# One order for five engines, searched anew: RWKV attention followed by a squared-ReLU MLP on one NeuronCore

## The chip, the cores and the metric

The kernel runs on 1 core of one Trainium2 chip. The metric is the device time of one execution, in microseconds (us). The core has five instruction streams that matter here: PE (TensorE, matmuls and transposes through matmul), DVE (VectorE), ACT (ScalarE), POOL (GpSimd) and SP (SyncE, which only starts DMAs). Each stream runs in order; semaphores hold an instruction until what it needs is done.

## The reference

Four sequences of 768 tokens, 8 heads of 48 channels, go through a linear attention with a decayed state, and the result (3072 tokens of 384 channels) through an MLP with a squared ReLU:

```python
for t in range(S):
    cur = np.einsum('bhd,bhe->bhde', u[None] * kt, vt)
    y[:, :, t] = np.einsum('bhd,bhde->bhe', rt, state + cur)
    state = wt[:, :, :, None] * state + np.einsum('bhd,bhe->bhde', kt, vt)
...
h = x @ w_in            # 384 x 2048
r = np.maximum(h, 0.0)
g = r * r
return g @ w_out        # 2048 x 384
```

## The kernel before, in words

The 3072 tokens are cut into 12 steps of 256 tokens, three to a sequence. A step s is written as a set of words, and each word issues one operation (or a few of one kind) on one engine. The order of all 864 words is written out by hand, in the string ORDER (L17), and a loop at the end of the kernel (L598) issues them one after the other. So ORDER fixes, for each engine, the order of its own instructions; between engines only the data and the buffers decide. A word reads `name.step.index`; `=A`, `=V` or `=G` behind it puts it on ACT, DVE or POOL, and `:n` names the PSUM bank or banks that it writes.

The words of one step, in the order of the data:

- ld (L172): DMAs of w, r, k, v into a ring of four steps; `ld.g.i` and `ld.g.o` (L188, L194) load the four chunks of the two MLP weights in f32, and cast (L200) makes them bf16.
- ww, rw, kw, ku, qp (L262 to L302): elementwise products of f32 tiles in SBUF, two tensor operands each; q (L306) sums over channels; lw (L268) takes a logarithm; v, vs, qs (L272, L281, L311) are copies that rearrange; vq (L316) is a product of two SBUF tiles.
- cum (L321, PE) sums the logarithms; al (L333), exp, ac (ACT) and rd (L351, DVE, rd.s.0 for r and rd.s.1 for k) turn them into decayed r and k. They read the bank that cum wrote, so that bank is free for the next user only after rd.
- The decayed r and k are transposed: in steps 0 to 3 by PE (tr, L370, copied out by rkt, L386), in steps 4 to 11 by a DMA transpose on SP (dtr, L397).
- p (L409, PE) and pm (L423, DVE, product with a mask out of PSUM): the scores; su (L436, PE), ts (L450), sn (L458, POOL): the state; y and yc (L475, L486, PE): the output; ysb (L499, DVE) adds vq to it.
- The output is transposed for the MLP: in steps 0 to 5 by PE and a copy (yt L509, xt L518), in steps 6 to 11 by a DMA transpose (dyt, L523).
- m1.s.g (L529, PE, six matmuls) makes 2 of 16 blocks of hidden channels; rl (L541, ACT or DVE) evicts them with the ReLU; sq (L549) squares two rl in SBUF; m2.s.c.q (L559, PE, four matmuls) adds a quarter of the hidden channels to 128 tokens of the result; os (L567) evicts it, store (L575) writes it out.
- warm (L579) are matmuls on a zero tile, issued while the first data comes.

PSUM has eight banks: att0 and att1 (two banks each, used by cum, p, su, y) and the four of `quad`, of which 0 and 1 are called `b` and 2 and 3 `m`. In the order before, m1 uses banks 2 and 3 in turn, and m2 banks 0 and 1. p, su and yc are matmuls on tiles of 64 x 64 of the array; y, m1, m2, tr, yt and cum use all of it.

Of the kernel before, what the change touches and what calls it, by code (L numbers as in the profile page):

```python
# [35 lines left out]
qp_.3=G ld.5.v m1_.2.3:2 os_.0.0=V rl_.2.0=V tr_.3.1:0 rl_.2.3=A tr_.3.0:1 rkt_.3.1=V v_.3=A ld.4.r m1_.2.4:3
ww_.4=G rkt_.3.0=V m2_.1.0.0:0 rl_.2.4=A q_.3 ww_.5=G p_.3.1:0 vs_.3.1=A ld.6.k su_.3:1 pm_.3.1 p_.3.0:m
m2_.1.0.1 ts_.3.0=A lw_.4 sn_.3.0 ld.5.k pm_.3.0 m2_.1.0.2 qs_.3=A m2_.1.1.0:1 sq_.2.0=A vq_.3=G ts_.3.1=V
m2_.1.0.3 ld.6.w cum_.4:0 m2_.1.1.1 ku_.4=G ac_.4 al_.4 store.0.1 m1_.2.5:2 os_.1.0=A v_.5=A yc_.3.1:1 y_.3:1
lw_.5 kw_.4=G m1_.2.2:3 ld.6.r ysb_.3=V rl_.2.5=A m2_.1.1.2 exp_.4 sn_.3.1 rl_.2.2=V yt_.3:0 rw_.4=G cum_.5:1  # L40
xt_.3=V m2_.1.1.3 vs_.4.0=A ac_.5 sq_.2.1=A qp_.4=G al_.5 m1_.3.0:2 rd_.4.1 v_.4=A m1_.3.3:3 rd_.4.0 dtr_.4.1
m2_.2.0.0:0 rl_.3.0=A rw_.5=G rl_.3.3=A m2_.2.0.1 os_.1.1=V exp_.5 q_.4 dtr_.4.0 su_.4:0 sq_.2.2=A m1_.3.4:2
kw_.5=G rd_.5.0 ww_.6=G m2_.2.1.0:1 rl_.3.4=A ts_.4.0=V sq_.2.3=A m1_.3.5:3 vs_.4.1=A rd_.5.1 sn_.4.0
m2_.2.1.1 store.1.0 ts_.4.1=V rl_.3.5=V ku_.5=G m1_.3.6:2 store.1.1 m2_.2.1.2 qs_.4=A ld.7.w ld.6.v rw_.6=G
p_.4.1:1 rl_.3.6=A p_.4.0:0 pm_.4.1 pm_.4.0 m2_.2.1.3 lw_.6 vq_.4=G m1_.3.1:3 m1_.3.2:2 rl_.3.1=A su_.5:1
dtr_.5.1 dtr_.5.0 vs_.5.1=G sq_.3.0=A rl_.3.2=V yc_.4.0:0 yc_.4.1:0 sn_.4.1 y_.4:0 os_.2.1=V sq_.3.1=A
m1_.3.7:3 ysb_.4=V ld.7.v m2_.2.0.2 rl_.3.7=A ld.8.w kw_.6=G vs_.5.0=G yt_.4:1 ld.7.k sq_.3.3=A m2_.2.0.3
xt_.4=V cum_.6:0 al_.6 m1_.4.4:2 qp_.5=G os_.2.0=A ac_.6 m1_.4.7:3 ts_.5.0=V exp_.6 rl_.4.4=V m2_.3.0.0:1
rl_.4.7=A rd_.6.1 m1_.4.6:2 rd_.6.0 m2_.3.0.1 dtr_.6.1 m2_.3.1.0:0 ku_.6=G qp_.6=G sq_.3.2=A rl_.4.6=A q_.5
dtr_.6.0 p_.5.0:1 p_.5.1:0 vs_.6.0=A m1_.4.5:3 sn_.5.0 m2_.3.0.2 qs_.5=G rl_.4.5=A pm_.5.1 pm_.5.0 vq_.5=G  # L50
m1_.4.1:2 m1_.4.3:3 rl_.4.3=A store.2.1 ld.8.v m2_.3.0.3 rl_.4.1=V ld.8.k v_.6=A ww_.7=G y_.5:0 q_.6 os_.3.0=A
ld.7.r m1_.4.0:3 store.0.0 ld.9.k ww_.8=G yc_.5.0:0 qs_.6=A su_.6:1 yc_.5.1:0 ysb_.5=V vs_.6.1=A ts_.6.0=V
m1_.4.2:2 ld.8.r m2_.3.1.1 rl_.4.0=V yt_.5:1 xt_.5=V sn_.6.0 lw_.7 vq_.6=G rl_.4.2=A p_.6.0:0 m2_.3.1.2
sq_.4.3=A store.2.0 pm_.6.0 m1_.5.2:3 ku_.7=G m1_.5.6:2 ts_.6.1=V yc_.6.1:0 sq_.4.0=A rl_.5.2=A p_.6.1:1
rl_.5.6=A m2_.3.1.3 kw_.7=G pm_.6.1 sq_.4.2=A m1_.5.4:3 rw_.7=G m1_.5.3:2 os_.3.1=V rl_.5.4=A y_.6:0 sn_.6.1
rl_.5.3=A cum_.7:1 kw_.8=G ysb_.6=V al_.7 m2_.4.0.0:1 vs_.7.1=A m1_.5.7:3 m1_.5.5:2 v_.7=G dyt_.6 sq_.4.1=A
rl_.5.7=V qp_.7=G rl_.5.5=V m2_.4.1.0:0 exp_.7 ld.9.w ld.9.v m2_.4.0.1 ac_.7 rd_.7.0 sq_.5.1=A m2_.4.0.2
ku_.8=G rd_.7.1 sq_.5.3=A dtr_.7.0 m2_.4.0.3 m1_.5.0:3 lw_.8 m1_.5.1:2 rw_.8=G rl_.5.0=V su_.7:0 q_.7
rl_.5.1=A cum_.8:1 dtr_.7.1 m1_.6.3:3 qs_.7=A m1_.6.5:2 rl_.6.3=V ld.10.w qp_.8=G ac_.8 sq_.5.0=A m2_.4.1.1
os_.4.0=V ts_.7.0=V ld.11.w sn_.7.0 m1_.6.4:3 rl_.6.5=A al_.8 ww_.9=G m2_.4.1.2 ld.9.r rl_.6.4=V exp_.8  # L60
# [574 lines left out]
```

## Time and profile before

| | us |
|---|---|
| three runs: median (lowest to highest) | 182.38 (181.91 to 182.72) |
| the profiled execution, its time | 182.57 |
| the profiled execution, its span (first to last instruction) | 180.8 |

| engine | busy us | share of the span |
|---|---|---|
| PE matmul | 171.2 | 95% |
| ACT | 132.4 | 73% |
| DVE | 129.7 | 72% |
| POOL | 122.8 | 68% |

The granted clock of TensorE is full over the whole span. A row of a timeline reads: start in us, duration, engine, line, operation, output<-inputs, shape, number of instructions, and in brackets the idle time ahead of it with what ended it. A matmul's recorded duration runs longer than the distance to the next start, since matmuls are pipelined; distances are read from start to start. A row of the groups reads: line, engine, operation, tiles, shape, count, then total busy us and mean ns of one, then the idle time ahead of the group and what ended most of it. In the chain of work that ended last, 33% of the span is m2 (L564) and 33% is m1 (L536).

### The profile page before, as it was taken

What the parts mean: (1) busy time and instruction counts of PE and PEld (TensorE: products, weight loads), DVE (VectorE), ACT (ScalarE), POOL (GpSimd) and SP (SyncE); (2) the same over time, 40 slices, a digit from 0 to 9 for tenths busy, and PEclk for the clock granted to TensorE, in tenths of its full rate; (3) what the DMA queues carried; (4) which work ended last, traced back from release to release, by engine and by line L of the source; (5) the groups of instructions that cost most, each with busy time, mean ns of one, the idle gap of its engine ahead of it and who ended that gap; (6) DMA issues with size and microseconds to landing.
All of it is one profiled execution on the core that took longest, in us unless ns stands there. A gap on an engine that the chain in (4) does not pass through costs nothing.

```text
span 180.8 us, 5682 instructions
## 1 busy us (share of the span) xinstructions
PE 171.2 (95%) x2382; PEld 123.2 (68%) x2385; DVE 129.7 (72%) x195; ACT 132.4 (73%) x235; POOL 122.8 (68%) x140
## 2 busy tenths in 40 slices
...
GB/s 147 270 261 232 221 369 350 340 332 302 228 271 217 280 228 215 208 218 255 270 137 237 197 287 101 303 141 143 190 106 244 92 47 0 92 151 22 0 87 130
DMA packets 78952, 35.81 MB, mean 198 GB/s; under 512 B 72144, under 2 KB 77392, under 8 KB 78928
## 3 DMA queue, kind: packets, MB, share of 16 engines
...
## 4 chain that ended last, share of the span: by engine, by line
PE 78%; SPq 10%; DMA 5%; ACT 4%; DVE 1%; issue 1%; ACTq 0%
PE bk L564 33%; PE m L536 33%; SPq L180 8%; DMA w_st<-in_moe_w_in_dram 5%; PE att L420 3%; PE att L483 3%; PE att L493 2%; PE att L446 1%; ACT gt L545 1%; PE bk L516 1%; PE att L328 1%; ACT wi_sb L202 1%; SPq L190 1%; SPq L207 1%; ACT gt L553 1%
## 5 line engine op out<-in xcount | busy, mean ns | idle before, releaser
L536 PE MATMUL m<-xT,wi_sb 128*128 128x256 bf16 x576 | 74.0, 273 | 0.8 <-ACT gt L545 0.7
L564 PE MATMUL bk<-wo_sb,gt 128*128 128x384 bf16 x384 | 72.0, 326 | 0.0
L536 PEld LDWEIGHTS <-wi_sb 128*128 128x128 bf16 x576 | 54.8, 98 | 12.5 <-issue 0.9
L564 PEld LDWEIGHTS <-gt 128*128 128x128 bf16 x384 | 36.9, 98 | 19.2
L545 ACT ACTIVATE gt<-m 128x512 f16<-128x512 f32 x56 | 32.9, 594 | 21.6 <-PE m L536 21.1
L553 ACT ACTIVATE gt<-gt 128x1024 bf16<-128x1024 f16 x42 | 43.3, 1051 | 1.4 <-DVE gt L547 1.1
L547 DVE TENSOR_SCALAR gt<-m 128x512 f16<-128x512 f32 x40 | 27.1, 687 | 9.6 <-PE m L536 9.3
L434 DVE TENSOR_TENSOR pmT<-att,mask 128x1024 bf16<-128x1024 f32 x20 | 23.9, 1218 | 3.9 <-PE att L420 3.9
L299 POOL TENSOR_TENSOR ku<-k_raw,u_bc 128x768 f32<-128x768 f32 x12 | 21.8, 1819 | 0.4 <-DMA u_bc<-in_u_dram 0.4
L304 POOL TENSOR_TENSOR ku<-ku,r_raw 128x768 f32<-128x768 f32 x11 | 20.6, 1877 | 0.2
L318 POOL TENSOR_TENSOR ku<-v_sh,qs 128x768 f32<-128x768 bf16 x11 | 16.2, 1477 | 4.9 <-ACT qs L279 4.8
L279 ACT CAST v_sh<-v_raw 64x384 bf16<-64x384 f32 x34 | 17.3, 508 | 0.4
L292 POOL TENSOR_TENSOR k_raw<-k_raw,w_raw 128x384 f32<-128x384 f32 x12 | 12.1, 1010 | 6.3 <-DMA k_raw<-in_k_dram 6.2
L461 POOL TENSOR_TENSOR S<-t_state,ac_buf 128x192 bf16<-128x192 f32 x20 | 10.2, 508 | 8.1 <-DVE t_state L456 5.7
L504 DVE TENSOR_TENSOR y_sb<-att,ku 128x768 bf16<-128x768 f32 x12 | 11.4, 954 | 5.5 <-PE att L483 1.7
L288 POOL TENSOR_TENSOR r_raw<-r_raw,w_raw 128x384 f32<-128x384 f32 x12 | 12.0, 997 | 3.6 <-DMA r_raw<-in_r_dram 3.6
L363 DVE TENSOR_TENSOR kdec_buf<-k_raw,att 128x768 bf16<-128x768 f32 x12 | 11.4, 950 | 3.5 <-ACT att L342 2.9
L360 DVE TENSOR_TENSOR rdec_buf<-r_raw,att 128x384 bf16<-128x384 f32 x24 | 12.2, 548 | 2.2 <-ACT ac_buf L348 1.1
L342 ACT ACTIVATE att<-att 128x768 f32<-128x768 f32 x12 | 9.6, 799 | 3.4 <-PE att L330 2.0
L571 ACT ACTIVATE o_sb<-bk 128x384 f32<-128x384 f32 x13 | 6.2, 484 | 7.3 <-PE bk L564 7.3
L309 DVE TENSOR_REDUCE q<-ku 128x16 f32<-128x768 f32 x12 | 11.3, 944 | 0.0
L581 PE MATMUL att<-warm 128*128 128x512 bf16 x27 | 8.9, 487 | 1.2 <-DVE half_ones L230 1.2
...
## 6 DMA issues: line engine op xcount, KB each, us to landing
...
```

The costliest lines, as they stand in the source:

```text
L180: nc.sync.dma_start(out=t[:, hs, at:at + 2, :].rearrange("p h j d -> p h (j d)"), in_=src[b, hs, i * T:(i + 1) * T, :].rearrange("h (p j) ...
L279: copy(out[j * Q:(j + 1) * Q, c], src[c * Q:(c + 1) * Q, :, j])
L299: tensor_mul("ku_", s, h)(tiles["ku", s][:, hs], raw["k", s][:, hs, 1:3, :], u_bc[:, hs, None, :].to_broadcast([C, n, 2, D]))
L304: tensor_mul("qp_", s, h)(ku, ku, raw["r", s][:, heads(h), 0:2, :])
L318: tensor_mul("vq_", s)(vq[:], tiles["vs", s][:], tiles["qs", s][:, :, :, None].to_broadcast([C, 2, H, D]))
L360: nc.vector.tensor_mul(rdec[0][:, ps, j, :, 0:D], x[:, :, j, :].rearrange("p (a e) d -> p a e d", e=2), dec.rearrange("p (a e) d -> p a e ...
L434: nc.vector.tensor_mul(pmT, ps_p[:].rearrange("p e (x t) -> p (e x) t", t=C), mk.to_broadcast([C, 8, C]))
L536: nc.tensor.matmul(ps1[:, j, :], wi_sb[:, n // 4, kk, n % 4 * 128:(n % 4 + 1) * 128], tiles["xT", s][:, :, kk, :], start=(kk == 0), stop=( ...
L545: nc.scalar.activation(rl, m1, AF.Relu, scale=RS)
L547: nc.vector.tensor_scalar(out=rl, in0=m1, scalar1=RS, scalar2=0.0, op0=ALU.mult, op1=ALU.max)
L553: nc.scalar.activation(gt, rl, AF.Square)
L564: nc.tensor.matmul(m2, gt[:, 4 * q + n, c * C:(c + 1) * C], wo_sb[:, 4 * q + n, :], start=(summed[s, c] == 1 and n == 0), stop=(summed[s, ...
```

## The change

Only the string ORDER is changed. It holds the same 864 words before and after: the same operations on the same tiles, the same 22 DMA transposes, the same loads and stores. The first 90 words are the same; behind them the sequence is another one, found by a search whose plan of the DMA engines also holds the fetches of instructions and the DMA transposes. Three things differ:

- the sequence of the words on every engine, SP's included;
- the banks: m1 and m2 now take any of the four quad banks (m1: 19, 26, 25 and 26 words on banks 0 to 3, before 0, 0, 48 and 48; m2: 6, 8, 5 and 5 sums, before 11, 13, 0 and 0), tr and yt too, and the quarters of an m2 sum come in any order;
- the engine of 107 words. To DVE go ku.5, ku.10, ku.11, kw.3, kw.8, rw.5, ww.10, vq.2 and vq.9 from POOL, v.5 from ACT, vs.2.1 from POOL, vs.8.0 and vs.11.0 from ACT, and the squares sq.0.0, sq.0.3, sq.2.3, sq.8.0 and sq.10.1 from ACT (sq.9.3 goes to ACT), and ts.3.0 from ACT. 22 rl go from ACT to DVE and 27 the other way, three rkt, two xt and, on balance, one os from DVE to ACT; five qs, four v and four vs go from ACT to POOL, two qs, three v and three vs from POOL to ACT, and cast.o.2 from POOL to ACT.

The diff, cut to the start, to two places in steps 6 to 11, and to the end. First the old lines of these places, then the new ones:

```diff
-ac_.2 cast.i.1=A rd_.2.1 warm_.10.1 tr_.2.0:1 sn_.1.0 p_.1.0:0 ku_.2=G ts_.1.1=V yc_.1.1:1 tr_.2.1:0
-cast.i.0=A pm_.1.0 ld.0.o m1_.0.3:2 ld.3.w rkt_.2.1=V m1_.0.2:3 vq_.1=G rkt_.2.0=V y_.1:1 rl_.0.3=A yc_.1.0:1
-rl_.0.2=V p_.2.0:0 m1_.0.1:2 ld.1.o ysb_.1=V cast.i.2=G m1_.0.0:3 rl_.0.1=A pm_.2.0 yt_.1:0 ld.3.r rl_.0.0=A
-m1_.0.5:2 v_.2=A xt_.1=V qp_.2=G sn_.1.1 m1_.0.4:3 rl_.0.5=A p_.2.1:1 su_.2:b sq_.0.0=A rl_.0.4=V ld.2.o
-m1_.1.4:2 cast.i.3=G ts_.2.0=V pm_.2.1 m1_.1.5:3 rl_.1.4=A q_.2 sn_.2.0 m1_.1.3:2 rl_.1.5=A ld.3.o vs_.2.1=G
-vs_.2.0=A yc_.2.0:0 yc_.2.1:0 rl_.1.3=V m1_.1.6:3 cast.o.0=G qs_.2=A m1_.1.0:2 ld.3.k rl_.1.6=V sq_.0.2=A
-y_.2:0 rl_.1.0=V m1_.1.1:3 vq_.2=G m1_.1.7:2 rl_.1.1=V ld.3.v m2_.0.1.0:0 sq_.1.2=A rl_.1.7=V sq_.0.1=A
-cast.o.1=G m1_.1.2:3 rl_.1.2=A ysb_.2=V m1_.0.7:2 ld.4.w ww_.3=G yt_.2:1 rl_.0.7=V m1_.0.6:3 xt_.2=V m2_.0.1.1
-sq_.1.1=A rl_.0.6=V ld.5.w m1_.2.6:2 cast.o.2=G lw_.3 sq_.1.0=A rl_.2.6=A cum_.3:1 sq_.1.3=A rw_.3=G al_.3
...
-store.3.0 m2_.5.1.0:1 sq_.5.2=A rd_.8.1 ts_.7.1=V sn_.7.1 m1_.6.0:2 vs_.7.0=G vs_.9.1=A rd_.8.0 m2_.4.1.3
-m2_.5.1.1 kw_.9=G rl_.6.0=A dtr_.8.0 p_.7.1:0 v_.8=A p_.7.0:1 vq_.7=G pm_.7.1 m1_.6.1:3 m2_.5.1.2 rl_.6.1=A
-pm_.7.0 ku_.9=G m2_.5.1.3 sq_.6.0=A lw_.9 m1_.6.6:2 dtr_.8.1 store.3.1 q_.8 yc_.7.0:0 v_.9=A yc_.7.1:0
-rl_.6.6=V rw_.9=G su_.8:1 y_.7:0 os_.5.1=A ts_.8.0=V m1_.6.2:3 ysb_.7=V os_.4.1=A cum_.9:1 m1_.6.7:2 al_.9
-dyt_.7 m2_.5.0.0:1 rl_.6.2=V exp_.9 ww_.10=G rl_.6.7=V m2_.5.0.1 ac_.9 ld.10.r rd_.9.1 sq_.6.1=A sq_.6.2=A
-sn_.8.0 qp_.9=G ld.10.k qs_.8=G store.4.1 m2_.5.0.2 ld.10.v rd_.9.0 m2_.5.0.3 m2_.6.1.0:0 vs_.8.1=G sq_.6.3=A
-dtr_.9.0 vs_.8.0=A p_.8.0:m p_.8.1:0 pm_.8.0 su_.9:1 m2_.6.1.1 ts_.9.0=A pm_.8.1 m2_.6.1.2 lw_.10 m1_.7.4:2
-rw_.10=G os_.5.0=V m1_.7.0:3 rl_.7.4=V sn_.9.0 vq_.8=G yc_.8.1:0 dtr_.9.1 yc_.8.0:0 rl_.7.0=V y_.8:0 m1_.7.1:2
...
-os_.6.0=A y_.9:0 sq_.7.3=A rl_.8.2=V yc_.9.1:0 rw_.11=G su_.10:1 m2_.7.1.0:1 sq_.7.2=A ts_.10.0=V ysb_.9=V
-m2_.7.1.1 rl_.8.4=A ku_.11=G q_.10 m1_.8.7:3 dyt_.9 m1_.8.1:2 rl_.8.7=V cum_.11:0 dtr_.10.1 kw_.11=G sn_.10.0
-rl_.8.1=A m2_.7.1.2 al_.11 m1_.8.0:3 exp_.11 ld.11.v qs_.10=G ts_.10.1=V sn_.10.1 vq_.10=G m1_.8.6:2 rl_.8.0=A
-store.6.0 rd_.11.0 m2_.7.1.3 rl_.8.6=A rd_.11.1 m1_.9.4:3 sq_.8.0=A ac_.11 dtr_.11.0 m1_.9.1:2 qp_.11=G
-rl_.9.4=V sq_.8.2=A m2_.7.0.1 os_.7.1=V p_.10.1:1 sq_.8.1=A p_.10.0:0 pm_.10.1 store.5.0 dtr_.11.1 store.7.1
-m1_.9.0:3 v_.11=G pm_.10.0 vs_.11.1=G m2_.8.1.0:1 rl_.9.0=A rl_.9.1=A m2_.8.1.1 sq_.8.3=V m1_.9.5:3 m2_.7.0.2
-m2_.7.0.3 os_.7.0=A yc_.10.0:1 yc_.10.1:1 rl_.9.5=V su_.11:0 y_.10:1 m1_.9.2:2 ysb_.10=V m1_.9.6:3 rl_.9.2=A
...
+warm_.10.1 yc_.1.0:0 sn_.1.0 cast.i.1=A p_.1.0:b vq_.1=G ts_.1.1=V pm_.1.0 tr_.2.0:2 ld.3.w m1_.0.2:3
+rkt_.2.0=A rl_.0.2=A rd_.2.1 yc_.1.1 ld.1.o y_.1 m1_.0.3:3 ysb_.1=V sn_.1.1 rl_.0.3=V tr_.2.1:1 yt_.1:2
+cast.i.0=A m1_.0.0:0 m1_.0.1:3 xt_.1=A ac_.2 ku_.2=G qp_.2=G rkt_.2.1=V p_.2.0:1 rl_.0.1=A q_.2 ld.0.o
+p_.2.1:0 cast.i.2=G m1_.1.2:2 pm_.2.1 m1_.1.3:3 qs_.2=G ld.3.k m1_.1.5:1 v_.2=A rl_.1.2=A ld.3.r vs_.2.1=V
+su_.2:0 rl_.1.3=A ld.2.o ts_.2.0=V rl_.0.0=A vs_.2.0=A m1_.1.4:2 rl_.1.4=A rl_.1.5=A sq_.1.2=A pm_.2.0
+m1_.1.0:3 rl_.1.0=V sn_.2.0 cast.i.3=G yc_.2.1:0 ww_.3=G cast.o.1=G yc_.2.0 y_.2 lw_.3 m1_.0.5:1 rl_.0.5=A
+m1_.0.6:3 rl_.0.6=A m1_.0.7:2 cum_.3:1 vq_.2=V ysb_.2=V yt_.2:0 sq_.0.0=V xt_.2=V cast.o.0=G m1_.0.4:1
+rl_.0.7=V sq_.0.3=V al_.3 m1_.1.1:3 rl_.0.4=A m1_.1.7:0 rl_.1.7=V m1_.2.7:2 rl_.1.1=A rw_.3=G ld.3.o sq_.0.1=A
+m1_.2.0:3 exp_.3 rl_.2.7=A rl_.2.0=V m1_.1.6:1 m1_.2.4:0 sq_.1.1=A ld.3.v rl_.1.6=V m1_.2.1:2 kw_.3=V
+rl_.2.4=A rd_.3.1 m2_.0.0.0:3 rl_.2.1=A m1_.2.5:1 sq_.0.2=A rl_.2.5=A ld.4.w m2_.0.0.1 m2_.0.1.1:0 m1_.2.3:1
+rd_.3.0 tr_.3.1:2 m2_.0.1.0 rl_.2.3=V cast.o.2=A tr_.3.0:1 cast.o.3=V m2_.0.1.2 sq_.1.3=A m2_.0.0.2 m2_.0.0.3
...
+dyt_.6 rw_.8=G qp_.7=G q_.7 qs_.7=G sq_.5.2=A store.4.1 m1_.6.4:0 su_.7:1 m1_.6.3:2 os_.4.0=A m1_.6.1:1
+rl_.5.6=A store.3.0 rl_.6.3=A ld.8.v dtr_.7.0 m1_.6.0:3 m1_.6.7:2 rd_.8.0 ww_.9=G kw_.8=V ts_.7.0=V sn_.7.0
+rd_.8.1 dtr_.7.1 lw_.9 rl_.6.1=V ts_.7.1=V m1_.6.2:1 rl_.6.4=A yc_.7.1:0 p_.7.0:1 yc_.7.0 rl_.6.0=V dtr_.8.0
+rl_.6.2=V pm_.7.0 rl_.6.7=A p_.7.1:m sq_.5.3=A sq_.5.1=A m1_.6.5:0 pm_.7.1 ku_.8=G sq_.6.1=A vs_.8.1=A
+dtr_.8.1 v_.8=G m2_.5.1.0:1 m2_.5.1.1 su_.8:1 qp_.8=G q_.8 sn_.7.1 p_.8.0:m y_.7 ts_.8.0=V vq_.7=G m2_.5.1.3
+pm_.8.0 qs_.8=A rl_.6.5=A ld.10.w cum_.9:1 m2_.5.1.2 sn_.8.0 ysb_.7=V ld.11.w m1_.6.6:3 m2_.5.0.0:0 rl_.6.6=A
+sq_.6.0=A yc_.8.1:0 al_.9 os_.5.1=V yc_.8.0 p_.8.1:m ww_.10=V rw_.9=G vs_.8.0=V ld.9.v ld.9.k pm_.8.1
+m2_.5.0.1 m2_.6.0.0:1 m2_.5.0.3 dyt_.7 y_.8 sq_.6.2=A m2_.6.0.1 lw_.10 exp_.9 vs_.9.1=A vq_.8=G ysb_.8=V
...
+rd_.10.0 store.4.0 dtr_.9.0 rl_.7.7=A m1_.7.1:1 dtr_.9.1 qp_.9=G sn_.9.0 ts_.9.1=V p_.9.0:1 os_.6.1=A
...
+rl_.7.0=A sq_.7.0=A sn_.9.1 dtr_.10.0 yc_.9.1 ld.11.r qp_.10=G rl_.8.4=A su_.10:b dtr_.10.1 kw_.11=G store.5.1
+q_.10 qs_.9=G rl_.7.4=A sq_.7.2=A ts_.10.0=V m2_.7.1.1 vq_.9=V ac_.11 al_.11 m2_.7.0.1:2 sn_.10.0 exp_.11
+ts_.10.1=V m2_.7.0.3 m2_.7.0.2 m1_.8.5:0 m2_.7.0.0 rw_.11=G ld.11.v m1_.8.6:1 ysb_.9=V vs_.10.0=G rl_.8.5=A
+vs_.10.1=A sq_.8.2=A p_.10.0:0 rd_.11.1 rd_.11.0 os_.7.0=A p_.10.1:1 m2_.7.1.2 rl_.8.6=A m1_.8.3:0 m1_.8.2:2
+v_.11=A m1_.8.1:1 ku_.11=V pm_.10.1 rl_.8.1=A pm_.10.0 yc_.10.1:1 dtr_.11.1 dyt_.9 qs_.10=G sn_.10.1 su_.11:0
...
+m2_.11.1.3 store.10.0 store.9.0 sq_.11.1=A m2_.11.0.1 m2_.11.0.0 os_.11.0=A store.11.0 m2_.11.1.1 m2_.11.1.2
 os_.11.1=A store.11.1
```

86 lines of the change are left out of this document (42 added, 44 removed).

## Prediction

> **What bounds the kernel now.** I read the page first (busy shares, costliest groups), then the timeline of TensorE (PE) for the distances between starts, then the timelines of the engines that feed it at the places where those distances are not the usual ones.
>
> ```profile
> span 180.8 us, 5682 instructions
> PE 171.2 (95%) x2382; PEld 123.2 (68%) x2385; DVE 129.7 (72%) x195; ACT 132.4 (73%) x235; POOL 122.8 (68%) x140
> ...
> L547 DVE TENSOR_SCALAR gt<-m 128x512 f16<-128x512 f32 x40 | 27.1, 687 | 9.6 <-PE m L536 9.3
> L434 DVE TENSOR_TENSOR pmT<-att,mask 128x1024 bf16<-128x1024 f32 x20 | 23.9, 1218 | 3.9 <-PE att L420 3.9
> L299 POOL TENSOR_TENSOR ku<-k_raw,u_bc 128x768 f32<-128x768 f32 x12 | 21.8, 1819 | 0.4 <-DMA u_bc<-in_u_dram 0.4
> ...
> L504 DVE TENSOR_TENSOR y_sb<-att,ku 128x768 bf16<-128x768 f32 x12 | 11.4, 954 | 5.5 <-PE att L483 1.7
> L363 DVE TENSOR_TENSOR kdec_buf<-k_raw,att 128x768 bf16<-128x768 f32 x12 | 11.4, 950 | 3.5 <-ACT att L342 2.9
> L360 DVE TENSOR_TENSOR rdec_buf<-r_raw,att 128x384 bf16<-128x384 f32 x24 | 12.2, 548 | 2.2 <-ACT ac_buf L348 1.1
> ...
> L309 DVE TENSOR_REDUCE q<-ku 128x16 f32<-128x768 f32 x12 | 11.3, 944 | 0.0
> ```
>
> PE is busy 95% of the span. Its timeline (start, duration, instructions) shows that this is real work at a fixed pace:
>
> ```profile
> 26.54 0.62 PE L376 MATMUL bk<-ident,kdec_buf 128*128 128x128 bf16 x8
> 27.00 1.47 PE L536 MATMUL m<-xT,wi_sb 128*128 128x256 bf16 x12
> 28.31 0.56 PE L483 MATMUL att<-v_sh,pmT 128*128 128x48 bf16 x16
> 28.80 0.31 PE L493 MATMUL att<-S,rT 64*64 64x48 bf16 x16
> 28.95 0.40 PE L420 MATMUL att<-rT,kT 64*64 64x128 bf16 x16
> 30.05 1.47 PE L536 MATMUL m<-xT,wi_sb 128*128 128x256 bf16 x12 [0.70 <-ACT gt L545]
> 31.35 0.50 PE L516 MATMUL bk<-ident,y_sb 128*128 128x128 bf16 x6
> 31.70 1.48 PE L536 MATMUL m<-xT,wi_sb 128*128 128x256 bf16 x12
> 33.11 0.43 PE L420 MATMUL att<-rT,kT 64*64 64x128 bf16 x16
> 33.36 0.42 PE L446 MATMUL bk<-v_bf,kdec_buf 64*64 64x48 bf16 x16
> 33.71 2.33 PE L536 MATMUL m<-xT,wi_sb 128*128 128x256 bf16 x18
> ...
> 36.34 1.49 PE L536 MATMUL m<-xT,wi_sb 128*128 128x256 bf16 x12
> 37.66 0.56 PE L483 MATMUL att<-v_sh,pmT 128*128 128x48 bf16 x16
> 38.07 1.47 PE L536 MATMUL m<-xT,wi_sb 128*128 128x256 bf16 x12
> 39.37 0.81 PE L564 MATMUL bk<-wo_sb,gt 128*128 128x384 bf16 x4
> 40.02 1.47 PE L536 MATMUL m<-xT,wi_sb 128*128 128x256 bf16 x12
> ...
> 124.30 0.81 PE L564 MATMUL bk<-wo_sb,gt 128*128 128x384 bf16 x4
> 125.19 0.81 PE L536 MATMUL m<-xT,wi_sb 128*128 128x256 bf16 x6
> ...
> 170.10 7.31 PE L564 MATMUL bk<-wo_sb,gt 128*128 128x384 bf16 x44
> ```
>
> From start to start an m1 word (six matmuls) takes 0.65 us (38.07 to 39.37 for two), an m2 word 0.65 (39.37 to 40.02), a p word 0.25 (33.11 to 33.36), a su word of 16 matmuls 0.35 (33.36 to 33.71), yt 0.35, y 0.41 (37.66 to 38.07), yc 0.15 (28.80 to 28.95). Going from a full-array word to one on 64 rows costs 0.09 more (31.70 to 33.11 is 1.41, two m1 words are 1.31); I take the same for the way back. From 27.00 to the last m2 words nearly all starts follow at these distances. The two exceptions shown are 28.95 to 30.05, 1.10 where a p word and a way back need 0.34, so a wait of 0.76, and 124.30 to 125.19, 0.89 instead of 0.65. The last matmul ends at 177.41 (170.10 + 7.31); one eviction and one store fill the rest. So PE bounds it. An order with the same 864 words can win only by starting the MoE work earlier, dropping these waits, or changing array mode less often, and it loses wherever PE is made to wait.
>
> **The start.** The wait at 28.95 hangs on ACT:
>
> ```profile
> 25.02 0.18 ACT L348 ACTIVATE ac_buf<-att 128x8 f32<-128x8 f32 x1 [0.98 <-DVE rdec_buf L360]
> 25.10 1.47 ACT L202 CAST wi_sb<-w_st 128x1536 bf16<-128x1536 f32 x1
> 28.03 1.47 ACT L202 CAST wi_sb<-w_st 128x1536 bf16<-128x1536 f32 x1 [1.46 <-DMA w_st<-in_moe_w_in_dram]
> 29.40 0.59 ACT L545 ACTIVATE gt<-m 128x512 f16<-128x512 f32 x1
> ```
>
> Today cast.i.1 stands behind ac_.2, which sat idle 0.98 us, until 25.02, for rd_.2.0. In the new order it stands right behind vs_.1.0, so it starts between 24.04 and 25.02 (as its data has landed) and ends between 25.5 and 26.5. The first m1 word stands ahead of tr_.2.1 instead of behind both tr words, so it starts at 25.7 at the earliest instead of 27.00. That lead is not kept: the next m1 pair needs cast.i.0, whose data lands at 28.03 in any order, so PE waits until 29.5. Today the word after that starts at 30.05, because its bank waits for rl_.0.3 (29.40), which is queued behind the cast; the new order uses bank 0, which is free, and has yt_.1 (0.35) done by then but p_.2.0 (0.25 + 0.09) not. It is ahead by 0.5. Walking on with these durations to the point where 11 m1 words and y_.2 are issued (38.07 today), I meet short waits of 0 to 0.3 each at y_.2 (for pm_.2.0) and m1_.0.5 (for rl_.1.5 behind four other ACT words): the point comes at 37.3 to 37.8, a gain of 0.3 to 0.8. The next DVE words, vq_.2 (moved from POOL), ysb_.2 and sq_.0.0 (moved from ACT), feed yt_.2 and can give up to 0.5 of it back. I take -0.4, with -0.8 and +0.2 as ends.
>
> **Mode changes and old waits.** Behind the first m1 word today's order changes mode 22 times each way, the new one 21 times: 2 x 0.09 = -0.2. The 0.24 us at 124.30 and crumbs of its size go with their neighbours; the new order has neighbours of its own. -0.3 for the old, +0.3 for new ones of the kind.
>
> **Work moved to DVE.** Against today DVE takes over three ku, two kw, two vq, one rw, one ww and one v from POOL or ACT, three vs and net four sq, and gives up net five rl, three rkt and two xt. By the rows above and their like that is some 8 us more on DVE and 10 less on POOL; DVE's 129.7 us bear it on average, but not everywhere. An operation starts some 0.08 before the recorded end of the one ahead, so I count duration less 0.08. Two places just fit:
>
> Place A, m1_.6.2 to y_.8. PE needs three m1 and eight m2 words (7.15), four p (1.0), four yc (0.6), y_.7 (0.41), su_.8 and cum_.9 (0.6 by the su row) and six mode changes (0.54): 10.3. From the end of m1_.6.2 (0.65, and some 0.2 for its result) DVE must do rl_.6.2 (0.61), four pm (4 x 1.14 to 1.2, 4.7), q_.8 (0.86), ysb_.7 (0.87) and five short words, ts_.8.0, al_.9, os_.5.1, ww_.10, vs_.8.0, at L360's 0.47 each (2.35): 9.4, and y_.8 waits for the last pm. 0.85 + 9.4 against 10.3: it fits by nothing. 0 to +0.5; I take +0.2.
>
> Place B, su_.10 to su_.11. Up to p_.10.1 PE needs su_.10 (0.35), five m2 and two m1 (4.55), p_.10.0 and a mode change (0.34): 5.2. DVE must do, once su_.10 has ended (0.55), ts_.10.0, al_.11, ts_.10.1 (at most L360's 0.47 each, 1.4), vq_.9, ysb_.9 (0.87), rd_.11.1 (0.87) and rd_.11.0 (0.93), which reads the bank that p_.10.1 overwrites: 4.1 and vq_.9. vq_.9 costs 0.74 to 1.5 (next part), so p_.10.1 comes 0 to 1.0 late. Then ku_.11 (0.87) and both pm_.10 (2.3) stand before su_.11, with 3.2 us of PE work beside them: no slack to win it back. +0.6, ends 0 and +1.1.
>
> The price of a moved operation has one example:
>
> ```profile
> 18.22 1.60 DVE L318 TENSOR_TENSOR ku<-v_sh,qs 128x768 f32<-128x768 bf16 x1
> ...
> 18.02 0.99 POOL L266 TENSOR_TENSOR ww<-w_raw 128x384 f32<-128x384 f32 x1
> 18.97 2.52 POOL L304 TENSOR_TENSOR ku<-ku,r_raw 128x768 f32<-128x768 f32 x1
> ```
>
> vq_.0 on DVE took 1.60 us. It began at 18.22 while POOL's ww ran until 19.01, and ended at 19.82; POOL's next operation took 2.52 where the same ku shape one line up in the kernel (L299) averages 1.82. That reads as DVE standing still until 19.01 and working 0.81, and POOL standing still meanwhile. The Trainium skill, "SBUF — State Buffer", section "🔬 SBUF: two separate sides", states it as a rule: the port pair that DVE and GpSimd share is an exclusive lock, and a DVE operation with two SBUF inputs holds it against a GpSimd operation that reads SBUF. The trace agrees, by the 0.79 us and the 0.7 us just read. By that rule every moved kw, ku, rw, ww, vq and each early sq pays this whenever POOL is busy; nothing in the sum above needs the rule.
>
> **DMA.** The transposes of rdec, kdec and y stay the same 22 words on SP; the data that they move is the same.
>
> ```profile
> L403 SPq DMA_TRANSPOSE kT<-kdec_buf x8: 1260/1350/3636, 62.7 to 138.1; - x8
> ...
> DMA to landing us min/median/max: 3.2/3.9/6.2
> ```
>
> Neither PE wait above is shown as one for a transpose, so moving them has little to win. They come nearer to their use: between rd_.8.1 and p_.8.0 stand 3.9 us of PE words where 11 stood. On my walk rd_.8.1 runs about 1.3 us ahead of its place, and 1.35 (issue) to 3.9 fits. Zero, with a loss as a rival. The end (two m2, os on ACT, store) is the same: zero.
>
> Sum: -0.4 - 0.2 - 0.3 + 0.3 + 0.2 + 0.6 = +0.2 us. The profiled execution took 182.57 us, which makes 182.8; it lies 0.19 above the median of the three runs, 182.38, so I forecast 182.6 against that median. Less than 0.5%, 0.9 us, is about what a measurement of this kernel can tell from no change.
>
> **Rivals.** (1) Faster: places A and B hold, as DVE runs a little ahead and vq_.9 meets an idle POOL. Then the start gives its full 0.8: -0.8 - 0.2 - 0.3 + 0.1 = -1.2, 181.2. For it: POOL has 10 us less to do and is idle more often; against it: A and B have no slack. No more is to be had, since the first w_in chunks land when they land. (2) Slower, by the shared port: the moved words on paths without slack (vq_.2, sq_.0.0, ww_.10, vq_.9, ku_.11) each wait for the rest of a POOL operation. The example paid 0.79 and the longest POOL operation of the page is 1.8; two such waits are in my sum, three more at 0.5 to 0.8 make +1.5 to +2.4: 184.5. It decides once PE's waits before yt_.2, y_.8 and su_.11 pass 1 us together beyond the sum. (3) Slower, by transposes: with the 6.2 us of the slowest landing instead of 3.9, dtr_.8.1 comes 1 to 2 us after PE wants p_.8.0, and dtr_.9.1, some 6 us ahead of p_.9.0, nearly so: +1.5, 184.1. For it: the queue is shared with loads; against it: the median. (4) That the change doesn't do what it says, since fetches and transposes cost PE nothing today, is what I forecast.
>
> **How the numbers follow.** Forecast 0.38 (own range 181.6 to 183.3), rival 1 0.25, rival 2 0.20, rival 3 0.17. Faster by over 0.5% is rival 1, 0.25; slower the two others, 0.37; the forecast is the middle, 0.38. The range 181.0 to 184.5 leaves out the lower third of rival 1 (0.08) and the upper half of rival 2 (0.10).
>
> **What would show it.** Right: m1 starting at 25.7 to 26.5, its second pair at 29.5, PE waits of 0.2 to 1 us before y_.8 and p_.10.1 or su_.11 with DVE full ahead of them, PE else dense to the end. Rival 2 shows as moved DVE operations of 1.2 us and more beside stretched POOL ones; rival 3 as PE waiting at p_.8 or p_.9 with DVE idle; rival 1 as neither. A stall of several us at a place not named here would make the prediction wrong.

## The result, and the profile after

The changed kernel takes 183.01 us (median of 20 runs, 182.14 to 184.40), the kernel before 182.44 (20 runs beside it, 181.59 to 183.58): a ratio of 1.0043, 95% interval 1.0026 to 1.0060. That is some 0.6 us slower, and the interval leaves 1 out; it is less than the 0.5% that the prediction called no change. The forecast was 182.6.

The profiled execution of the changed kernel took 182.58 us and is one of its faster ones, so its page is read with that in mind. The rows that answer to those of before:

```profile
span 180.4 us, 5711 instructions
...
PE 170.9 (95%) x2382; PEld 122.7 (68%) x2385; DVE 137.6 (76%) x209; ACT 129.7 (72%) x222; POOL 117.0 (65%) x143
...
L318 POOL TENSOR_TENSOR ku<-v_sh,qs 128x768 f32<-128x768 bf16 x9 | 13.3, 1477 | 9.7 <-ACT qs L279 6.3
L299 POOL TENSOR_TENSOR ku<-k_raw,u_bc 128x768 f32<-128x768 f32 x9 | 16.4, 1822 | 0.0
```

PE has the same work. DVE is busy 7.9 us more and POOL 5.8 less; two vq and three ku have left POOL. The timeline of PE at the start (start, duration, instructions):

```profile
24.60 0.71 PE L376 MATMUL m<-ident,rdec_buf 128*128 128x128 bf16 x8
25.35 0.83 PE L536 MATMUL m<-xT,wi_sb 128*128 128x256 bf16 x6
...
29.08 0.83 PE L536 MATMUL bk<-xT,wi_sb 128*128 128x256 bf16 x6 [0.37 <-ACT wi_sb L202]
...
36.40 1.47 PE L536 MATMUL m<-xT,wi_sb 128*128 128x256 bf16 x12
38.34 0.25 PE L326 MATMUL att<-half_ones,lw_buf 128*128 128x2 bf16 x4 [0.47 <-ACT lw_buf L270]
```

The first m1 starts at 25.35 instead of 27.00, the second pair at 29.08. Eleven m1 words and y_.2 are issued at 37.06 (the row at 36.40 holds two m1 words, and the second starts there), where the kernel before stood at 38.07: a lead of 1.0. Then cum_.3 comes at 38.34 where 37.71 was due (36.40 and two m1 words, 1.31): 0.63 of the lead is gone at one wait. The timelines of POOL, DVE and ACT show why:

```profile
34.59 1.47 POOL L202 CAST wi_sb<-w_st 128x1536 bf16<-128x1536 f32 x1
36.02 1.72 POOL L266 TENSOR_TENSOR ww<-w_raw 128x384 f32<-128x384 f32 x1
...
35.71 1.17 DVE L318 TENSOR_TENSOR ku<-v_sh,qs 128x768 f32<-128x768 bf16 x1
37.85 1.83 DVE L555 TENSOR_TENSOR gt<-gt 128x1024 bf16<-128x1024 f16 x1
...
37.77 0.52 ACT L270 ACTIVATE lw_buf<-ww 128x384 bf16<-128x384 f32 x1 [0.98 <-POOL ww L266]
```

ww_.3 took 1.72 us on POOL, where others of its shape take 0.99 in the kernel before, and it began beside vq_.2, which the change had put on DVE. Without the 0.72 lw_.3 would have been done before 37.71. A second case, with the order of the two engines turned round:

```profile
59.06 1.81 POOL L304 TENSOR_TENSOR ku<-ku,r_raw 128x768 f32<-128x768 f32 x1
...
59.45 1.98 DVE L555 TENSOR_TENSOR gt<-gt 128x1024 bf16<-128x1024 f16 x1
```

sq_.2.3, moved from ACT to DVE, began at 59.45 and ended 0.56 us after POOL's qp_.4 (60.87), where a free square takes 0.68: as these times read, it stood still until POOL was done. m2_.2.0.3 waits 0.16 us for it. The Trainium skill, "SBUF — State Buffer", section "🔬 SBUF: two separate sides", calls the port pair of DVE and GpSimd an exclusive lock, held for a whole instruction by the one that starts first; these rows agree.

The two places that the prediction feared:

```profile
111.80 1.14 PE L564 MATMUL bk<-wo_sb,gt 128*128 128x384 bf16 x6
112.78 0.56 PE L483 MATMUL att<-v_sh,pmT 128*128 128x48 bf16 x16
...
114.75 0.81 PE L536 MATMUL m<-xT,wi_sb 128*128 128x256 bf16 x6
115.78 0.99 PE L564 MATMUL bk<-wo_sb,gt 128*128 128x384 bf16 x5 [0.22 <-ACT gt L553]
...
131.98 0.82 PE L536 MATMUL bk<-xT,wi_sb 128*128 128x256 bf16 x6
132.73 0.70 PE L420 MATMUL att<-rT,kT 64*64 64x128 bf16 x32
133.36 0.82 PE L564 MATMUL m<-wo_sb,gt 128*128 128x384 bf16 x4
...
128.31 0.35 DVE L456 TENSOR_TENSOR t_state<-S,bk 128x192 f32<-128x192 bf16 x1 [0.19 <-PE bk L446]
128.58 0.95 DVE L318 TENSOR_TENSOR ku<-v_sh,qs 128x768 f32<-128x768 bf16 x1
...
132.86 0.95 DVE L299 TENSOR_TENSOR ku<-k_raw,u_bc 128x768 f32<-128x768 f32 x1
...
128.81 1.09 POOL L461 TENSOR_TENSOR S<-t_state,ac_buf 128x192 bf16<-128x192 f32 x1 [0.61 <-DVE t_state L456]
```

y_.8 (112.78) starts after six m2 matmuls, 0.98, with no gap. p_.10.0 and p_.10.1 take 0.63 together where 0.59 is their pace. Places A and B just fit. The DVE rows are ts_.10.0 (L456), vq_.9 (L318) and ku_.11 (L299): POOL had been idle for 0.61 us when sn_.10.0 (L461) began at 128.81, so vq_.9 met no POOL operation at its start. It was sn_.10.0 that took 1.09 instead of 0.51. The wait of this stretch is another one: m2_.6.0.3 at 115.78 instead of 115.40, 0.38 us for sq_.6.3 on ACT. So the profile shows three waits that the change brought in, 0.63 + 0.16 + 0.38 = 1.17, more than the lead, and yet its last matmul ends 0.28 us earlier than before (177.13 against 177.41). That contradicts a median that is 0.57 longer, and the experiments begin there.

### The profile page after: what moved, and what is told of

Its sections match the earlier page's. It is cut to its first block, busy times and chain, and to the rows that moved or that the text cites. A ratio compares the mean times of both kernels' runs of the same rounds, so it can differ in the third digit from the quotient of the medians.

```text
span 180.4 us, 5711 instructions
## 1 busy us (share of the span) xinstructions
PE 170.9 (95%) x2382; PEld 122.7 (68%) x2385; DVE 137.6 (76%) x209; ACT 129.7 (72%) x222; POOL 117.0 (65%) x143
## 4 chain that ended last, share of the span: by engine, by line
PE 76%; SPq 10%; DMA 5%; ACT 4%; POOL 2%; issue 1%; DVE 0%; POOLq 0%
PE bk L564 19%; PE m L536 16%; PE bk L536 16%; PE m L564 14%; SPq L180 8%; DMA w_st<-in_moe_w_in_dram 5%; PE att L420 2%; PE att L483 2%; ACT gt L553 2%; PE att L446 2%; PE att L493 1%; POOL ww L266 1%; ACT wi_sb L202 1%; PE att L328 1%; POOL wi_sb L202 1%
## 5 line engine op out<-in xcount | busy, mean ns | idle before, releaser
L564 PE MATMUL bk<-wo_sb,gt 128*128 128x384 bf16 x224 | 42.4, 326 | 0.2 <-ACT gt L553 0.2
L536 PE MATMUL m<-xT,wi_sb 128*128 128x256 bf16 x306 | 39.7, 273 | 0.0
L553 ACT ACTIVATE gt<-gt 128x1024 bf16<-128x1024 f16 x38 | 39.2, 1054 | 0.4
L536 PE MATMUL bk<-xT,wi_sb 128*128 128x256 bf16 x270 | 35.5, 273 | 0.4 <-ACT wi_sb L202 0.4
L564 PE MATMUL m<-wo_sb,gt 128*128 128x384 bf16 x160 | 30.3, 326 | 0.0
L545 ACT ACTIVATE gt<-bk 128x512 f16<-128x512 f32 x31 | 18.2, 593 | 16.1 <-PE bk L536 16.0
L545 ACT ACTIVATE gt<-m 128x512 f16<-128x512 f32 x30 | 17.7, 595 | 8.3 <-PE m L536 8.0
L434 DVE TENSOR_TENSOR pmT<-att,mask 128x1024 bf16<-128x1024 f32 x16 | 19.2, 1217 | 2.2 <-PE att L420 2.1
L547 DVE TENSOR_SCALAR gt<-m 128x512 f16<-128x512 f32 x21 | 14.3, 685 | 7.2 <-PE m L536 7.1
L318 POOL TENSOR_TENSOR ku<-v_sh,qs 128x768 f32<-128x768 bf16 x9 | 13.3, 1477 | 9.7 <-ACT qs L279 6.3
L299 POOL TENSOR_TENSOR ku<-k_raw,u_bc 128x768 f32<-128x768 f32 x9 | 16.4, 1822 | 0.0
L461 POOL TENSOR_TENSOR S<-t_state,ac_buf 128x192 bf16<-128x192 f32 x20 | 11.6, 578 | 6.9 <-DVE t_state L456 5.0
```

Source lines behind the costliest of these rows:

```text
L299: tensor_mul("ku_", s, h)(tiles["ku", s][:, hs], raw["k", s][:, hs, 1:3, :], u_bc[:, hs, None, :].to_broadcast([C, n, 2, D]))
L318: tensor_mul("vq_", s)(vq[:], tiles["vs", s][:], tiles["qs", s][:, :, :, None].to_broadcast([C, 2, H, D]))
L434: nc.vector.tensor_mul(pmT, ps_p[:].rearrange("p e (x t) -> p (e x) t", t=C), mk.to_broadcast([C, 8, C]))
L536: nc.tensor.matmul(ps1[:, j, :], wi_sb[:, n // 4, kk, n % 4 * 128:(n % 4 + 1) * 128], tiles["xT", s][:, :, kk, :], start=(kk == 0), stop=( ...
L545: nc.scalar.activation(rl, m1, AF.Relu, scale=RS)
L547: nc.vector.tensor_scalar(out=rl, in0=m1, scalar1=RS, scalar2=0.0, op0=ALU.mult, op1=ALU.max)
```

## The experiments

**Both kernels again.** Nothing is edited.

> The changed kernel once more, nothing edited. In its first profile PE stands still for 2.6 us behind 24 us, at places that add up to about the 2.3 us of the kernel before, and its span is 0.4 us shorter; but its median over 20 runs is 0.6 us longer. Theory M (margins): the first profile caught a lucky execution; the new order lets more PE words start within 0.3 us of their last input (59 against 41), so that a DMA or an eviction that is a little later makes PE wait. Then a profile whose time is near 183.0 or above shows 0.4 us or more of further PE waits behind 24 us, at words that had little margin (p_.7.0 and p_.9.0 had 0.32 and 0.43 us after their DMA transposes, y_.8, p_.10.1 and su_.11 none). Rival S (start): executions differ ahead of the first m1 word; then the first m1 word comes later than 25.35 by about what the time is longer, and the waits behind it stay at 2.6. Rival N (noise): the times of this repeat lie at a ratio within 0.2% of 1.

> The changed kernel a third time, for one more profile. M: as for the second, the waits differ from profile to profile at words of small margin, and their sum goes with the span. S: the first m1 word moves and the waits do not.

> The kernel before once more, nothing edited. Its ratio to itself, 1.000 within 0.2%, says what a measurement of five rounds can tell. M: its second profile has PE waits behind 24 us of 2.3 with changes of 0.3 or less, since its DMA transposes land 0.84 us and more ahead of their use. S: the first m1 word moves.

The changed kernel took 183.04 us (182.45 to 183.76), ratio 1.0021 (1.0002 to 1.0041); the kernel before against itself 0.9996 (0.9975 to 1.0016). The waits of PE behind 24 us, each worked out from start to start against the prediction's distances:

| profile | time | time less span | waits in all | ahead of 36 us | cum_.3 | m2_.2.0.3, m2_.6.0.3 | rest |
|---|---|---|---|---|---|---|---|
| before | 182.57 | 1.78 | 2.3 | 2.0 | 0 | 0 | 0.3 |
| before again | 182.84 | 1.78 | 2.6 | 2.3 | 0 | 0 | 0.3 |
| changed | 182.58 | 2.14 | 2.6 | 1.3 | 0.63 | 0.54 | 0.1 |
| again_a | 183.76 | 2.14 | 3.7 | 1.9 | 0.63 | 0.54 | 0.7 |
| again_b | 183.31 | 2.14 | 3.1 | 1.6 | 0.63 | 0.56 | 0.3 |

N's bound of 0.2% is just passed. M holds in part: the waits go with the time. But most of the spread sits at the start, at m1_.0.2 and m1_.0.0, which wait for casts of w_in chunks (cast.i.1 began at 23.82 us right behind vs_.1.0, and in the two repeats at 24.29 and 24.35, as its data landed); m1 came at 25.35, 25.82 and 25.88. The rest differs too:

```profile
88.79 0.39 PE L536 MATMUL m<-xT,wi_sb 128*128 128x256 bf16 x2
89.46 0.60 PE L536 MATMUL m<-xT,wi_sb 128*128 128x256 bf16 x4 [0.28 <-issue]
```

```profile
121.92 1.47 PE L536 MATMUL bk<-xT,wi_sb 128*128 128x256 bf16 x12
123.67 0.65 PE L420 MATMUL att<-rT,kT 64*64 64x128 bf16 x32 [0.28 <-DMA kT<-kdec_buf]
```

In again_a (first) PE stood still inside m1_.5.1 with nothing to wait for, 0.45 in all; in again_b (second) p_.9.0 waited for its transpose, 0.35.

The third column was not looked for. Time less span is 1.78 in both profiles of the kernel before and 2.14 in all three of the changed one. The other executions, whose spans are on record to 0.1 us, say the same: 1.7 to 1.9 for the kernel before, 2.1 to 2.2 for the changed one. So 0.36 of the 0.57 us between the medians lies ahead of the first or behind the last instruction, and 0.21 inside (183.01 - 2.14 against 182.44 - 1.78).

**ww_.3 earlier.**

```diff
-m1_.1.0:3 rl_.1.0=V sn_.2.0 cast.i.3=G yc_.2.1:0 ww_.3=G cast.o.1=G
+m1_.1.0:3 rl_.1.0=V ww_.3=G sn_.2.0 cast.i.3=G yc_.2.1:0 cast.o.1=G
```

> The changed kernel with ww_.3 on POOL moved ahead of sn_.2.0, into the 1.52 us in which POOL stood idle. In the profile of the changed kernel ww_.3 took 1.72 us instead of 0.99, beside vq_.2 on DVE, and lw_.3 and cum_.3 waited for it: PE lost 0.63 us. Theory P (a wait on the path that sets the end): PE waits at cum_.3 for less than 0.1 us and the time falls by 0.4 to 0.6, to a ratio of about 1.000 to 1.002 to the kernel before. Rival Q (the lead is taken back): the words behind cum_.3 wait for evictions and casts in its place (m1_.0.4, m1_.1.1 and m1_.1.7 had margins of 0.18, 0.35 and 0.11), and less than 0.2 us is won.

184.81 us (184.01 to 185.08), ratio 1.0111 (1.0085 to 1.0137): a miss of over 2 us.

```profile
35.23 1.00 POOL L266 TENSOR_TENSOR ww<-w_raw 128x384 f32<-128x384 f32 x1 [2.61 <-DMA w_raw<-in_w_dram]
36.18 0.51 POOL L461 TENSOR_TENSOR S<-t_state,ac_buf 128x192 bf16<-128x192 f32 x1
36.63 2.20 POOL L202 CAST wi_sb<-w_st 128x1536 bf16<-128x1536 f32 x1
...
36.30 1.21 DVE L318 TENSOR_TENSOR ku<-v_sh,qs 128x768 f32<-128x768 bf16 x1
...
36.74 0.44 PE L493 MATMUL att<-S,rT 64*64 64x48 bf16 x32 [1.16 <-POOL S L461]
38.89 1.48 PE L536 MATMUL m<-xT,wi_sb 128*128 128x256 bf16 x12 [0.54 <-POOL wi_sb L202]
```

The idle time on POOL was no room: ww_.3's data lands at 35.2, and sn_.2.0 and cast.i.3 stood behind it. yc_.2.1 lost 1.23, m1_.0.6 0.70. The run tells one thing well: away from vq_.2 ww_.3 takes 1.00, and the cast that is now beside vq_.2 takes 2.20 instead of 1.47. The extra 0.72 goes with the neighbour, not with the operation.

**cum_.3 later.** PE, ACT and DVE get other work ahead of it.

```diff
-lw_.3 m1_.0.5:1 rl_.0.5=A m1_.0.6:3 rl_.0.6=A m1_.0.7:2 cum_.3:1 vq_.2=V ysb_.2=V yt_.2:0 sq_.0.0=V xt_.2=V cast.o.0=G m1_.0.4:1 rl_.0.7=V
+m1_.0.5:1 rl_.0.5=A m1_.0.6:3 rl_.0.6=A lw_.3 m1_.0.7:2 m1_.0.4:1 vq_.2=V ysb_.2=V rl_.0.7=V yt_.2:0 cum_.3:1 xt_.2=V sq_.0.0=V cast.o.0=G
```

> The changed kernel with the 0.63 us at cum_.3 covered instead of hurried: on PE m1_.0.4 and yt_.2 go ahead of cum_.3, on ACT lw_.3 behind rl_.0.5 and rl_.0.6, on DVE rl_.0.7 and xt_.2 ahead of sq_.0.0. Theory P: this wait is on the path in every execution (0.63 in all three profiles), so the wait at cum_.3 falls below 0.1 and the time by 0.5 to 0.6 us, to about 182.5. Rival Q: the words behind it (m1_.1.7 and m1_.2.7, which wait for xt_.2 and rl_.0.7 on DVE) wait in its place and less than 0.2 is won.

183.20 us (182.88 to 184.81), ratio 1.0057 (1.0032 to 1.0082): nothing won. Q holds in the time; the word that waits is not one of those that it named.

```profile
38.43 0.50 PE L516 MATMUL bk<-ident,y_sb 128*128 128x128 bf16 x6
38.76 0.24 PE L326 MATMUL att<-half_ones,lw_buf 128*128 128x2 bf16 x4
...
43.01 0.82 PE L536 MATMUL bk<-xT,wi_sb 128*128 128x256 bf16 x6 [0.55 <-DVE gt L547]
...
39.53 2.36 DVE L555 TENSOR_TENSOR gt<-gt 128x1024 bf16<-128x1024 f16 x2
41.82 0.55 DVE L335 SCALAR_TENSOR_TENSOR att<-att,lw_buf 128x384 f32<-128x384 f32 x1
42.29 0.67 DVE L547 TENSOR_SCALAR gt<-bk 128x512 f16<-128x512 f32 x1
```

cum_.3 no longer waits, but m1_.2.4 does, 0.71 for rl_.1.7, which stands behind two squares that the change moved to DVE.

**Three small waits.** m2_.6.0.3 goes behind m2_.6.0.2, m2_.2.0.3 behind m2_.1.1.2, and on SP store.4.0 behind dtr_.9.1.

> The changed kernel with three words moved: m2_.6.0.3 behind m2_.6.0.2 (it waited 0.38 us for sq_.6.3 in all three profiles), m2_.2.0.3 behind m2_.1.1.2 (0.16 for sq_.2.3, which took 1.98 us on DVE), and on SP store.4.0 behind dtr_.9.1 (p_.9.0 waited 0.35 us in one profile of three). Theory P: these waits go and nothing takes their place, -0.5 to -0.7 us, about 182.5. Rival Q: the sums that end later, os and the squares behind them, hold up a bank, and less than 0.2 is won.

184.63 us (183.19 to 185.15), ratio 1.0113 (1.0087 to 1.0139). The profiled execution took 183.19, the shortest of the six; what makes the median another 1.4 us longer is not shown. In it the three waits are gone, and a new chain is there:

```profile
122.24 0.49 ACT L571 ACTIVATE o_sb<-m 128x384 f32<-128x384 f32 x1 [1.27 <-DMA out_dram<-o_sb]
...
125.27 0.25 PE L326 MATMUL att<-half_ones,lw_buf 128*128 128x2 bf16 x4 [0.32 <-ACT lw_buf L270]
...
128.27 0.43 PE L446 MATMUL bk<-v_bf,kdec_buf 64*64 64x48 bf16 x31 [0.60 <-ACT gt L545]
```

The rows that are stored have four buffers. os_.6.1 reuses that of os_.4.0, so it waits for store.4.0, and with it all that ACT has behind it: 0.48 at cum_.11 and 0.81 at su_.10.

**Three operations back on POOL.** vq_.9, ku_.11 and ww_.10 get =G, at the same places.

> The changed kernel with vq_.9, ku_.11 and ww_.10 back on POOL, at the same place in the order. The prediction priced the places that they are in (m1_.6.2 to y_.8, su_.10 to su_.11) at +0.8 us of waits for DVE. If that price is there, the time falls by about 0.8 to 182.2. By the three profiles it isn't: PE waits for less than 0.1 at p_.10.1 and su_.11 and for nothing at y_.8, and the three operations took 0.95, 0.95 and 0.55 us on DVE, not the 1.2 and more of a shared port; then the time stays within 0.2 of 183.0. It rises by 0.5 and more if qs_.10, sn_.10.1 and qp_.11, which are queued behind them on POOL, come late for yc_.11 and ysb_.10.

183.97 us (182.70 to 186.37; 183.87 without the highest, which the ratio leaves out), ratio 1.0067 (1.0041 to 1.0093). No gain of 0.8: that price was not there. The time rose by 0.9, as the last sentence of the text allows, but not by the words named there. The profiled execution took 184.64; in it place B gets worse:

```profile
130.03 1.47 POOL L318 TENSOR_TENSOR ku<-v_sh,qs 128x768 f32<-128x768 bf16 x1
131.46 0.51 POOL L461 TENSOR_TENSOR S<-t_state,ac_buf 128x192 bf16<-128x192 f32 x1
...
132.00 0.35 DVE L456 TENSOR_TENSOR t_state<-S,bk 128x192 f32<-128x192 bf16 x1 [0.48 <-POOL S L461]
...
135.07 0.43 PE L420 MATMUL att<-rT,kT 64*64 64x128 bf16 x16 [0.22 <-DVE rdec_buf L360]
```

On POOL vq_.9 stands ahead of sn_.10.0, ts_.10.1 waits for that, rd_.11.0 behind it is late, and p_.10.1 loses 0.40. So vq_.9 belongs on DVE there. Another 0.87 us of this profile arose ahead of the edits (m1_.5.2 at 95.54, behind os_.4.1), before any of the three words had run.

**The start alone.** The first 162 words but three, then the order before; ten words on other quad banks.

> The start of the changed kernel (its first 162 words but ww_.3, lw_.3 and cast.o.1, to m1_.0.6 and its rl) and behind it all other words in the order and on the engines of the kernel before (m1_.0.4, m1_.1.6, m1_.1.1, m1_.1.7 and six m1 of step 2 on other quad banks, ysb_.2 ahead of rl_.1.7, xt_.2 ahead of rl_.0.7). Over the profiles y_.2 and 11 m1 words are issued at 37.4 us in the changed kernel and at 38.2 in the kernel before. If the start is the good half of the change and the rest the bad one, the lead of 0.8 is kept to the end: 181.7, a ratio of 0.994 to 0.997 to the kernel before. Rival: casts and loads that land at fixed times take the lead back ahead of 45 us, by PE waits at m2_.0.1.0, yt_.2 or cum_.3, and the time is 182.3 or above.

184.03 us (183.69 to 184.94), ratio 1.0088 (1.0065 to 1.0111): the rival.

```profile
38.91 1.47 POOL L202 CAST wo_sb<-w_st 128x1536 bf16<-128x1536 f32 x1 [2.42 <-DMA w_st<-in_moe_w_out_dram]
...
42.86 0.51 PE L516 MATMUL bk<-ident,y_sb 128*128 128x128 bf16 x6 [0.96 <-DVE y_sb L504]
```

The new start loads the w_out chunks in another sequence (1 ahead of 0), and the old rest casts chunk 0 first: POOL stands 2.42, vq_.2 comes late behind it, and yt_.2 loses 1.13. It shows that start and rest hang together by their loads, and is no clean price of either half. One number is clean: with the old rest, time less span is 1.80, as before (182.2 span, 184.01).

**The two swaps alone, and six buffers alone** (bufs=6 in the pool of o_sb, its order untouched). "The run before last" in the first text is the run with the three small waits.

> The changed kernel with the two swaps of the run before last's three edits alone: m2_.6.0.3 behind m2_.6.0.2, m2_.2.0.3 behind m2_.1.1.2; store.4.0 stays. With store.4.0 moved, both waits were gone, but os_.6.1 on ACT stood 1.27 us for a store that freed its buffer, and cum_.11 and the word behind su_.10 lost 1.3 us to it. Theory P: with the store left where it is, only the win is left, 0.38 + 0.16: 182.5 against 183.0. Rival M (margins): a win of 0.5 us ahead of 116 us brings PE nearer to transposes and stores that land when they land (p_.7.0, p_.9.0, os_.6.1), half or more of it is lost there, and the median stays at 182.8 or above.

> The changed kernel with six buffers for the rows that are stored instead of four; its order is untouched. In its profiles os_.4.1 on DVE stood 0.5 to 0.6 us for the store that freed its buffer, and m1_.5.2, which waits for that bank, had 0.3 us of margin; in the run with three operations back on POOL that wait grew to 1.7 and cost PE 0.87. In the two profiles of the kernel before no eviction waits for a store. Theory M: such waits make the upper half of the times; the wait is gone from the profile, the highest times fall (184.4 and 184.1 among 20), and the median falls by 0.1 to 0.3, to 182.7 to 182.9. Rival: the store wait stays within its margin in most executions, and the median stays within 0.1 of 183.0.

Swaps: 183.23 us (182.20 to 183.57), ratio 1.0033 (1.0011 to 1.0055). The waits of 0.54 are gone from its profile, but the time isn't shorter, and lies where M said. Six buffers: 183.20 us (182.55 to 183.71), ratio 1.0036 (1.0019 to 1.0053). The eviction of the first row below (changed kernel) is freed in the second (six buffers), and the median stays: that wait was within its margin. The third row, also of the run with six buffers, is p_.7.0 waiting 0.41 for its transpose.

```profile
93.37 0.56 DVE L573 TENSOR_SCALAR o_sb<-m 128x384 f32<-128x384 f32 x1 [0.58 <-DMA out_dram<-o_sb]
```

```profile
92.86 0.56 DVE L573 TENSOR_SCALAR o_sb<-m 128x384 f32<-128x384 f32 x1
...
103.85 0.43 PE L420 MATMUL att<-rT,kT 64*64 64x128 bf16 x16 [0.25 <-DMA kT<-kdec_buf]
```

**All together, twice.** First: swaps, six buffers, cum_.3 later, and rl_.1.7 ahead of sq_.0.3. Second: also al_.3 ahead of sq_.0.0, sq_.0.3 behind rd_.3.0, store.4.0 behind dtr_.9.1. On DVE:

```diff
-xt_.2=V sq_.0.0=V rl_.1.7=V sq_.0.3=V al_.3 rl_.2.0=V rl_.1.6=V kw_.3=V rd_.3.1 rd_.3.0
+xt_.2=V al_.3 sq_.0.0=V rl_.1.7=V rl_.2.0=V rl_.1.6=V kw_.3=V rd_.3.1 rd_.3.0 sq_.0.3=V
```

> All that the runs showed to be on the path, put together: the two swaps, six buffers for the stored rows, and the cover of cum_.3 (m1_.0.4 and yt_.2 ahead of it on PE, lw_.3 behind rl_.0.5 and rl_.0.6 on ACT), now with rl_.1.7 ahead of sq_.0.3 and al_.3 on DVE, since in the run with cum_.3 later m1_.2.4 lost 0.71 us to rl_.1.7, which stood behind two squares of 2.36 us together. Theory P: the waits of 0.63, 0.38 and 0.16 go: 183.0 - 1.2 = 181.8, faster than the kernel before (182.45). Rival M: the words behind wait for data that lands at its own time, p_.7.0 and p_.9.0 for transposes above all, and the time stays at 182.4 or above.

183.94 us (182.95 to 185.06), ratio 1.0075 (1.0051 to 1.0099). The profiled execution, 183.19, is one of the faster ones; it has 1.26 us at one word:

```profile
44.27 0.81 PE L536 MATMUL m<-xT,wi_sb 128*128 128x256 bf16 x6 [1.09 <-ACT gt L545]
...
42.91 0.80 ACT L342 ACTIVATE att<-att 128x768 f32<-128x768 f32 x1 [1.44 <-DVE att L335]
...
42.33 0.55 DVE L335 SCALAR_TENSOR_TENSOR att<-att,lw_buf 128x384 f32<-128x384 f32 x1
```

m1_.2.1 waits for rl_.2.7 behind exp_.3 on ACT, that for al_.3 on DVE, that stood behind the squares. It is the wait of cum_.3, two engines further on.

> The combination of the run before with the wait that took the place of the others removed as well: there PE lost 1.26 us at m1_.2.1, which waited for rl_.2.7 on ACT behind exp_.3, and exp_.3 for al_.3 on DVE behind sq_.0.0, rl_.1.7 and sq_.0.3. Now al_.3 stands ahead of sq_.0.0, and sq_.0.3 behind rd_.3.0. Also store.4.0 goes behind dtr_.9.1, which with six buffers frees nothing late. Theory P: the waits between 37 and 45 us are gone (below 0.2 together), those at m2_.2.0.3, m2_.6.0.3 and p_.9.0 too, and PE waits behind 24 us for about 1.5 to 2.0 in all instead of 3.1: 181.8 to 182.2, a ratio of 0.996 to 0.999 to the kernel before. Rival M: what is won ahead of 45 us is taken back by words that wait for data landing at its own time, and the time stays at 182.5 to 183.

182.13 us (181.48 to 183.84), ratio 0.9984 (0.9957 to 1.0011): P's time. It is not told apart from the kernel before. It is some 0.9 us faster than the changed one: its interval lies below the 1.0026 to 1.0060 of the first twenty runs, and overlaps the 1.0002 to 1.0041 of the repeat only at the edge. In the profile (182.67) two rows of PE are its only large waits:

```profile
26.22 0.83 PE L536 MATMUL m<-xT,wi_sb 128*128 128x256 bf16 x6 [0.75 <-ACT wi_sb L202]
...
30.20 0.83 PE L536 MATMUL bk<-xT,wi_sb 128*128 128x256 bf16 x6 [0.77 <-ACT wi_sb L202]
```

Behind 31 us only 0.4 is lost in all; the rest waits for w_in chunks that land when they land. Its time less span is 2.13. So the median of its spans is 180.0 us where that of the kernel before, run beside it, is 180.6: inside the span this order is the faster one by 0.6, and more than half of that goes outside.

## Why the prediction came out right

The forecast, a change of less than 0.5%, held, and 183.01 lies in its range. That so little can't be measured did not hold: the loss of 0.43% is clear of noise in the first comparison, and just so in the repeat (1.0002 to 1.0041). The sum, +0.2, equals what the median lost inside the span (0.21), and that is luck: the terms came out otherwise, and the larger part of the loss is outside the span, where the sum had no term.

- **The start, -0.4.** Up to the point named (37.3 to 37.8 predicted) the three profiles give 37.06, 37.70 and 37.54, the two of before 38.07 and 38.36: a lead of about 0.8, the upper end. (First m1 at 25.35, 25.82 and 25.88, second pair at 29.08, 29.71 and 29.56; 25.7 to 26.5 and 29.5 were said. The cast that the pair waits for, said to have its data at 28.03 in any order, began between 27.55 and 28.32 in the five profiles.) What was to be given back was placed at yt_.2, with up to 0.5; it was 0.63, one word ahead of it, at cum_.3, by lw_.3 and ww_.3, which the prediction did not follow. Net about -0.2.
- **Mode changes, -0.2.** The new order does have one less each way; no run measured this by itself.
- **Old waits -0.3, new ones +0.3.** The old 0.24 went. The new ones are 0.54 in every profile (m2_.2.0.3, m2_.6.0.3), and up to 0.7 more in single ones. Undersized. That it matters little alone (the swaps won nothing that shows) fits M, but isn't settled.
- **Places A and B, +0.8.** Nothing at A, less than 0.1 at B: the lower ends. The step that failed is the size of two terms at B. The sum allowed up to 1.5 for vq_.9 and 0.47 for each of the two ts words; less the overlap of 0.08 they took 0.87 and 0.27. ku_.11 and ww_.10, 0.95 and 0.55 by the profile, came as counted. Undoing the moves cost 0.40 at p_.10.1.
- **Transposes, 0.** p_.8.0, which rival 3 named, does not wait for one; p_.7.0 and p_.9.0 do in some executions, 0.1 to 0.4, far from 1.5. The decayed k took longer to land than the 3.9 us counted on, with medians of 5.1, 5.1 and 4.2 in the three profiles, and still p_.8.0 had it in time.
- **Rival 2**, the shared port, is there as a mechanism: vq_.2 stretched ww_.3 by 0.72, and sq_.0.0 and sq_.2.3 took 1.83 and 1.98. It hit at cum_.3 rather than at su_.11, and on POOL's side; it was not enough for 184.5. Over the whole profile twelve POOL operations took over 0.08 us longer than the median of their shape in the kernel before, 5.6 us in all (5.5 in each repeat), where the kernel before has two, 1.2 us in all. Each of the twelve began while a DVE operation that reads only SBUF tiles was under way. The 4.4 us between the two sums account for POOL giving up 5.8 us and not the 10 that the prediction counted. Of PE's waits listed above only the one at cum_.3 hangs on one of the twelve. That the 0.72 is what makes cum_.3 late is read from the rows; no run took away the neighbour alone without other waits.
- **Rivals 1 and 4.** That A and B hold, rival 1's condition, came true, and its -1.2 did not, since the start gave back 0.63, new waits came and 0.36 went outside the span. Only with those walked out is a time near the kernel before reached again. That fetches and transposes cost PE nothing is nearly so: the kernel before lost nothing to a transpose in its two profiles.
- **The time around the span** was taken as fixed. It grew by 0.36, the larger part of the loss, and no run shows why.

So the change gave about what it promised at the start, lost most of it at waits that it made, the largest between 37 and 44 us and behind POOL and DVE, and pays 0.36 outside. That those waits cost the time is shown by the last run, which has them no more and is 0.9 us faster (its six buffers alone changed nothing); the 0.36 is measured, and its cause is open.
